# Decay totals with the pairs innermost, logs 16 places sooner, and the last turn's sums started 8 places sooner, in a fused HGRN2 and serf kernel

## The chip, the cores and the metric

The kernel runs on one core of one Trainium2 chip. The core has five engines with a queue of instructions each: TensorE (PE; its weight loads are shown apart as PEld) for matrix products, VectorE (DVE), ScalarE (ACT) and GpSimd (POOL) for elementwise work, and SyncE (SP), whose queue issues most of the transfers. An engine takes its queue strictly in order and waits at an instruction until what it needs is there. The metric is the device time of one execution in microseconds (us). Before the change it is 604.55 us, the median of three runs (603.59, 604.55 and 605.84).

## The reference

Two blocks follow each other. The first is a gated linear recurrence over 768 positions for 4 batches of 8 heads with 48 channels; its output, laid out as 3072 rows of 384, is the input of the second, a product with a 384 x 2048 matrix, an activation, and a product with a 2048 x 384 matrix. All values are 32-bit floats.

```python
f = 1.0 / (1.0 + np.exp(-f_logit))
for t in range(S):
    state = f[:, :, t, :, None] * state + np.einsum('bhd,bhe->bhde', k[:, :, t], v[:, :, t])
    y[:, :, t] = np.einsum('bhd,bhde->bhe', q[:, :, t], state)
...
h = x @ w_in
sp = np.maximum(h, 0.0) + np.log1p(np.exp(-np.abs(h)))
g = h * erf(sp)
return g @ w_out
```

## The kernel before

**Chunks.** The 3072 positions are 24 chunks of 128, each of two halves of 64 (`C`). A chunk's recurrence is turned into matrix products. The logits of f, one position per partition, are clamped (L392) and become logarithms, `log(1 + exp(-logit))`, by an exp (L400) and a ln (L401) on ACT; the two need another function table than the tanh of the activation, so the table is loaded ahead of them (L380) and the other one again at the next tanh (shown at L163 or L719). PE sums the logarithms over the positions of each half (L424, or L435 in four tiles). `decays` takes two exps of these sums on ACT (both L444): `dp`, the decay since the half's start, and its inverse, `kd`. DVE multiplies q by dp (L457) and k by kd (L464). PE transposes both (L484, L494), ACT and DVE copy the transposes out (L504, L124), PE forms the scores (L576) and the products of k and v (L565), the scores are masked (L601, L603), and PE forms the output (L650), which ACT copies out as input of the second block (L661).

**Totals.** The last position of each half of dp, 8 heads x 48 channels, is the decay over that half. The state needs it along the partitions: 64 rows for each head of a pair, four pairs side by side, as `Tall[:, g, c, :]` with 128 partitions and four values. `dp` is stored as [position, head, channel padded to 64]. For chunks 0 to 5 PE moves the totals over: `sum_totals` loads a pair of heads of dp as weights and multiplies them by two columns of the identity (L584), and DVE copies the result to Tall (L590). From chunk 6 on `send_totals` issues transfers on SP's queue, one for each pair and half, eight a chunk, each of 128 values of 4 bytes to 128 partitions (L451). DVE scales the state by Tall (L539, L542) and POOL copies it beside v (L547).

**Blocks and turns.** Two chunks are a block of 256 rows; there are 12. Blocks 0 to 2 and the loading and rounding of the weights are in an early part whose order is written out by hand (`EARLY`). From then on a loop over turns (`it` = 2 to 11) orders the work. A turn is a stream of PE's products, the places, counted as `s`. From turn 4 to turn 10 it has 104 places: first the 56 (`n_o`) of `project(it - 2)`, the second product of an earlier block, then the 48 (`n_h`) of `hiddens(it + 1)`, the first product of a later one (L765), in four groups of four 128-wide tiles. Each place is one product, two records in the profile. Turn 11 is `project` three times, 168 places. Whatever else is due at a place is issued after its product, to the queues of the engines.

**A product of a block.** `project` uses seven half-size products instead of eight (the Strassen and Winograd scheme), which need sums and differences of blocks of the hidden values: `sum_h`, four DVE operations (L803) a group, one for each `sum_step`. Its order: 12 places of products 1, 2, 6 for groups 0 and 1, 16 places of 5, 7, 3, 4, then 12 places of 1, 2, 6 for groups 2 and 3. Here, at place 40, ACT copies product 1 (L932) and DVE adds the pair 2 and 6 (L924), which ends the use of the first of two pairs of PSUM banks. After 16 more places of 5, 7, 3, 4 three more L924 end that of the second. The next product, or the first groups of the hidden values, takes these pairs of banks in turn and waits for them.

**The activation.** Each group of hidden values is copied out of PSUM by ACT (L777) and then goes through seven steps: exp (L160), two tanh terms (L163 twice), two multiplications on DVE (L168 twice), a last tanh (L719) and a multiplication on DVE (L722). `act_step` advances the two groups in work by one step each. Two buffers `e` exist, so the exp of a group waits for L722 of the group before the last. Act steps are issued at places with `s % 9` equal to 2 or 6 in turns 4 to 10 and at every third place in turn 11.

**What else a turn issues.** At places 67 and 103 a `burst` runs a chunk's PE work of the recurrence in one stretch, with its copies, exps and multiplications behind it, the totals, and then the loads of chunks further on. `load_f` for a block's logits is issued 20 places before the end of a turn, eight transfers (L259). In the next turn `clamp` is issued six places ahead of `logs`:

```python
loads, logits_at = {n - 20: it + 5}, {36: it + 4}
if it == 3:
    loads[6], logits_at = it + 4, {8: it + 3, 34: it + 4}
...
if logits_at.get(s + 6, n_blocks) < n_blocks:
    clamp(logits_at[s + 6], 0, CPB)
if logits_at.get(s, n_blocks) < n_blocks:
    logs(logits_at[s], 0, CPB)
```

There are 12 blocks, so the first of these lines takes effect in turns 4 to 7. The sums of groups 0 to 2 of a block are queued one turn ahead of its product, those of group 3 within it at place 20; in turn 11 the sums of the following block are queued at place 40 of a product (L1202).

Of the kernel before, what the change touches and what calls it, by code (L numbers as in the profile page):

```python
# [47 lines left out]
AF = mybir.ActivationFunctionType  # L48
ALU = mybir.AluOpType
# [21 lines left out]
P = 128  # L71
# [3 lines left out]
def kernel(  # L75
# [133 lines left out]
    dps = [fixed(f"dp{i}", [P, H, DP], pool=fix) for i in range(2)]  # L209
# [230 lines left out]
    def decays(g):  # L440
        ps = dTs.pop(g).rearrange("t n (h d) -> t n h d", d=D)
        for t, scale in ((dps[g % 2], -1.0), (kds[g % 2], 1.0)):
            out = t[:, :, 0:D].rearrange("t (n h) d -> t n h d", n=2)
            nc.scalar.activation(out=out, in_=ps, func=AF.Exp, scale=scale)  # L444

    def send_totals(g):
        dp = dps[g % 2]
        for c in range(2):
            end = C * (c + 1)
            for a in range(HP):  # L450
                nc.sync.dma_start(  # L451
                    out=Tall[:, g, c, a : a + 1],
                    in_=dp[end - 1 : end, 2 * a : 2 * a + 2, :].rearrange("o r d -> o (r d)"),
                )

    def times_q(g):
        nc.vector.tensor_tensor(  # L457
            out=qd[:, :, 0:D], in0=qns[g % NQ][:].rearrange("t (h d) -> t h d", d=D),
            in1=dps[g % 2][:, :, 0:D], op=ALU.mult,
        )  # L460
# [120 lines left out]
    def sum_totals(g):  # L581
        pairs = dps[g % 2][:].rearrange("t (a r) d -> t a (r d)", r=2)
        for a in range(HP):
            nc.tensor.matmul(  # L584
                totals[:, 2 * a : 2 * a + 2], lhsT=pairs[:, a, :], rhs=ident[:, C - 1 : P : C],
                start=True, stop=True,
            )
# [487 lines left out]
    with tc.manual_schedule():  # L1075
# [13 lines left out]
        for t in dps:  # L1089
            nc.vector.memset(t[:, :, D:DP], 1.0)  # L1090
# [53 lines left out]
        for it in range(2, n_blocks):  # L1144
# [3 lines left out]
            loads, logits_at = {n - 20: it + 5}, {36: it + 4}  # L1148
# [10 lines left out]
            for s, _ in enumerate(gen):  # L1159
# [28 lines left out]
                if it < 4:  # L1188
                    step = s % 7 in (1, 4)
                elif it == n_blocks - 1:  # L1190
                    step = s % 3 == 1
                else:
                    step = s % 9 in (2, 6)
# [5 lines left out]
                elif it > 2:  # L1199
                    if s == n - n_h and it < n_blocks - 1:  # L1200
                        to_sum.extend(sum_h(groups[it - 1, gi]) for gi in range(NS))
                    if it == n_blocks - 1 and s % n_o == 40 and s < 2 * n_o:  # L1202
# [5 lines left out]
                    elif s < n_o or s % 3 == 0 or it == n_blocks - 1:  # L1208
                        sum_step()
# [217 lines left out]
```

## Time and profile before

| what | before |
|---|---|
| median of three runs | 604.55 us |
| profiled execution: its time | 603.14 us |
| its span, first to last instruction | 601.4 us |
| mean granted clock of PE | 0.995 |
| PE busy | 581.5 us |
| DVE busy | 429.6 us |
| ACT busy | 382.9 us |
| POOL busy | 103.5 us |
| turns 4, 5, 6, 7 begin at | 230.35, 276.51, 323.20, 368.47 us |
| turn 11 begins at | 540.6 us |

The profile page is one execution. "Busy" is time with an instruction in work; matmuls overlap, so PE's share says how long products were in work, not how well the array was used. A wait is put down to the instruction whose end came last before the waiting one began. The chain of waits follows from the last instruction back to what released it. A line of the timeline has the start in us, the busy time in us, the engine, the line of the kernel, the operation, what it writes and reads, how many instructions were merged, and in brackets the idle time ahead and its releaser. In the list of the instructions that touch a tile, durations are minimum, median and maximum in ns. A place of the second product takes 0.329 us in steady state (18.40 us for 56), one of the first 0.44 us.

### The profile page before, as it was taken

The page shows a single profiled execution, that of the slowest core. Times are in us where ns is not written, and L with a number is a line of the kernel's source. Part 1 is how long each engine was busy: PE and PEld are TensorE (multiplying, and loading weights), DVE is VectorE, ACT ScalarE, POOL GpSimd, SP SyncE. Part 2 cuts the span into 40 slices and gives each one's busy share as a digit, 9 for nine tenths or more (in the row PEclk, how much of TensorE's full clock was granted, in tenths as well). Part 3 has the DMA queues.
Part 4 walks back from the last instruction along what each step waited for, and adds up shares of the span by engine and source line. Part 5 has one row for each costly group of instructions (what it writes and reads, how often), then busy time and mean ns, then how long its engine had stood idle before and what let it go on. Part 6 is the DMA issues. An engine that isn't in the chain of part 4 may idle for free.

```text
span 601.4 us, 14264 instructions
## 1 busy us (share of the span) xinstructions
PE 581.5 (97%) x5939; PEld 507.6 (84%) x5939; DVE 429.6 (71%) x705; ACT 382.9 (64%) x483; POOL 103.5 (17%) x119
## 2 busy tenths in 40 slices
PE   8999999998799999999999999999999999999996
PEld 7787888886455778889988989989989989989996
DVE  5689889976977487596786685697695775647551
ACT  6748859787746876875866766766566646366000
POOL 1230342220404011033031010022142020000000
PEclk9899999999999999999999999999999999999999
DMA  9789974206231241232332323221311000000000
GB/s 186 212 223 255 238 176 97 43 2 158 31 76 28 55 77 19 52 72 33 71 56 34 72 34 51 52 56 27 75 29 20 26 2 1 27 1 2 27 26 31
DMA packets 152678, 41.38 MB, mean 69 GB/s; under 512 B 144416, under 2 KB 147488, under 8 KB 152608
## 3 DMA queue, kind: packets, MB, share of 16 engines
q1 hardware_dynamic: 150384, 39.81, 30.4%
q8 instruction: 49, 0.80, 0.6%
q10 hardware_dynamic: 2224, 0.59, 0.4%
q14 instruction: 21, 0.17, 0.1%
HBM read 35.59 MB, written 4.72 MB: 67 GB/s over the span
## 4 chain that ended last, share of the span: by engine, by line
PE 73%; ACT 12%; DVE 6%; DMA 3%; issue 2%; SPq 2%; POOL 1%; ACTq 0%; DVEq 0%
PE hps L765 33%; PE ops L916 22%; PE ops L865 5%; PE y L650 3%; ACT x L163 3%; PE sc L576 2%; PE sc L565 2%; PE ps_t L494 1%; DMA vt<-in_v_dram 1%; PE ps_t L484 1%; DVE Hg L722 1%; SPq L451 1%; ACT e L160 1%; DVE e L168 1%; ACT Hg L777 1%
## 5 line engine op out<-in xcount | busy, mean ns | idle before, releaser
L765 PE MATMUL hps<-xT,w_in_sb 128*128 128x256 f32 x1152 | 257.5, 381 | 4.5 <-ACT Hg L777 2.8
L765 PEld LDWEIGHTS hps<-xT,w_in_sb 128*128 128x128 f32 x1152 | 216.3, 190 | 37.5 <-ACT Hg L777 3.6
L547 POOL COPY sv<-state 48x192 f32<-48x192 f32 x88 | 87.2, 991 | 337.1 <-DVE state L542 285.2
L168 DVE SCALAR_TENSOR_TENSOR e<-x,e 128x1024 f32<-128x1024 f32 x96 | 117.3, 1221 | 15.0 <-ACT x L163 14.6
L163 ACT ACTIVATE x<-Hg,serf_bias 128x1024 f32<-128x1024 f32 x88 | 97.2, 1138 | 0.2
L160 ACT ACTIVATE e<-Hg 128x1024 f32<-128x1024 f32 x44 | 46.5, 1057 | 67.1 <-DVE Hg L722 67.0
L916 PE MATMUL ops<-wT,Hg 128*128 128x192 f32 x320 | 77.7, 326 | 0.0
L777 ACT COPY Hg<-hps 128x1024 f32<-128x1024 f32 x44 | 44.4, 1009 | 44.6 <-PE hps L765 44.2
L722 DVE TENSOR_TENSOR Hg<-Hg,e 128x1024 f32<-128x1024 f32 x44 | 53.7, 1220 | 24.3 <-ACT e L719 24.3
L916 PE MATMUL ops<-wT,scratch 128*128 128x192 f32 x288 | 67.8, 326 | 0.9 <-DVE scratch L924 0.9
L916 PE MATMUL ops<-w_out_sb,Hg 128*128 128x192 f32 x320 | 65.8, 328 | 0.0
L924 DVE TENSOR_TENSOR scratch<-scratch,ops 128x384 f32<-128x384 f32 (+1 forms) x40 | 19.9, 498 | 52.8 <-ACT scratch L932 41.9
L916 PEld LDWEIGHTS ops<-wT,Hg 128*128 128x128 f32 x320 | 56.3, 190 | 0.1
L603 DVE TENSOR_TENSOR qA<-sc,tri 64x256 f32<-64x256 f32 x68 | 28.7, 422 | 36.5 <-PE sc L576 32.8
L916 PEld LDWEIGHTS ops<-w_out_sb,Hg 128*128 128x128 f32 x320 | 53.8, 190 | 0.5
L719 ACT ACTIVATE e<-e 128x1024 f32<-128x1024 f32 x48 | 50.3, 1048 | 2.8 <-DVE e L168 2.8
L916 PEld LDWEIGHTS ops<-wT,scratch 128*128 128x128 f32 x288 | 50.3, 190 | 1.1 <-issue 1.1
L916 PE MATMUL ops<-w_out_sb,scratch 128*128 128x192 f32 x132 | 32.2, 326 | 0.0
L504 ACT COPY qA<-ps_t 64x512 f32<-64x512 f32 x48 | 27.8, 579 | 4.3 <-PE ps_t L494 2.8
L932 ACT COPY scratch<-ops 128x192 f32<-128x192 f32 x10 | 3.2, 319 | 39.5 <-PE ops L916 39.4
L650 PEld LDWEIGHTS y<-qA,sv 128*32 128x32 f32 x1408 | 21.0, 110 | 8.3 <-issue 6.2
L650 PE MATMUL y<-qA,sv 128*32 128x64 f32 x1408 | 25.0, 221 | 1.0 <-POOL sv L547 0.9
(129 smaller groups left out, 666.8 us busy)
## 6 DMA issues: line engine op xcount, KB each, us to landing
qn<-in_q_dram SPq DMA_DIRECT2D x24, 192.0 KB, 3.9
kn<-in_k_dram SPq DMA_DIRECT2D x23, 192.0 KB, 3.8
vt<-in_v_dram SPq DMA_DIRECT2D x23, 192.0 KB, 3.4
out_dram<-scratch SPq DMA_DIRECT2D x11, 384.0 KB, 2.5
sv<-in_v_dram SPq DMA_DIRECT2D x84, 48.0 KB, 2.5
w_out_sb<-in_moe_w_in_dram SPq DMA_DIRECT2D x4, 768.0 KB, 7.5
Hg<-in_moe_w_in_dram SPq DMA_DIRECT2D x4, 768.0 KB, 6.1
scratch<-in_moe_w_out_dram SPq DMA_DIRECT2D x4, 768.0 KB, 7.2
```

Source lines behind the costliest of these rows:

```text
L160: nc.scalar.activation(out=dst[:], in_=h, func=AF.Exp)
L163: nc.scalar.activation(out=dst[:], in_=h, func=AF.Tanh, bias=serf_bias[:, i : i + 1], scale=SERF_KAB[i][0])
L168: nc.vector.scalar_tensor_tensor(out=e[:], in0=x[:], scalar=SERF_KAB[i][2], in1=e[:], op0=ALU.add, op1=ALU.mult)
L547: nc.gpsimd.tensor_copy(out=svs[g1 % NSV][rows(r), r, c1, :, PAD : PAD + D], in_=state[rows(r)])
L603: nc.vector.tensor_tensor(out=to, in0=sc[half(c), r], in1=tri1[half(c)].unsqueeze(1).broadcast_to((C, HP, C)), op=ALU.mult,)
L650: nc.tensor.matmul(y[M * i : M * (i + 1), kt, half(c)], lhsT=sv[:, r, c, a, o : o + M], rhs=qA[:, r, a, half(c)], start=(c == 0 and n == 0 ...
L719: nc.scalar.activation(out=e[0][:], in_=e[0][:], func=AF.Tanh, scale=SERF_C)
L722: nc.vector.tensor_tensor(out=h, in0=h, in1=e[0][:], op=ALU.mult)
L765: nc.tensor.matmul(hts[blk, gi][:, j, :], lhsT=w_in_sb[:, kt, ft * P : (ft + 1) * P], rhs=xTs[blk][:, kt, :], start=(kt == 0), stop=(kt == ...
L777: nc.scalar.copy(out=gr["h"], in_=hts.pop((blk, gi))[:])
L865: nc.tensor.matmul(ops[:, tt, 0:d_model], lhsT=gr["h"][:, j, tt * P : (tt + 1) * P], rhs=w_out_sb[:, ft, :], start=(ft == 0), stop=(ft == ...
L916: nc.tensor.matmul(place[n], lhsT=x[:, j, :], rhs=y, start=(gi == 0 and j == 0 and n in first), stop=(gi == n_g - 1 and j == 1), skip_grou ...
```

## The change

Three parts. First, `dp` is stored as [position, head of a pair, channel padded to 64, pair], the four pairs innermost. The totals of a half are then 128 x 4 values in the order of Tall, and one transfer of 16 bytes to each of 128 partitions moves them: two transfers a chunk instead of eight. The exp that writes dp (the first L444), the multiplication that reads it for q (L457) and the weight loads of `sum_totals` (L584) now step by four values (16 bytes) from one channel to the next; the padding is set to one as before. Second, in turns 4 to 7 `logs` is issued at place 20 and `clamp` at place 14, where it was 36 and 30. Third, in turn 11 the sums of the following block are queued at place 32 of a product, not 40, and no act steps are issued in the last eight of a product's 56 places; the sum steps have the same bar, which acts together with two other conditions in the same line.

```diff
-    dps = [fixed(f"dp{i}", [P, H, DP], pool=fix) for i in range(2)]
+    dps = [fixed(f"dp{i}", [P, 2, DP, HP], pool=fix) for i in range(2)]
...
     def decays(g):
-        ps = dTs.pop(g).rearrange("t n (h d) -> t n h d", d=D)
-        for t, scale in ((dps[g % 2], -1.0), (kds[g % 2], 1.0)):
-            out = t[:, :, 0:D].rearrange("t (n h) d -> t n h d", n=2)
-            nc.scalar.activation(out=out, in_=ps, func=AF.Exp, scale=scale)
+        ps = dTs.pop(g)
+        nc.scalar.activation(
+            out=dps[g % 2][:, :, 0:D, :].rearrange("t r d (n a) -> t n a r d", n=2),
+            in_=ps.rearrange("t n (a r d) -> t n a r d", r=2, d=D), func=AF.Exp, scale=-1.0,
+        )
+        nc.scalar.activation(
+            out=kds[g % 2][:, :, 0:D].rearrange("t (n h) d -> t n h d", n=2),
+            in_=ps.rearrange("t n (h d) -> t n h d", d=D), func=AF.Exp,
+        )
 
     def send_totals(g):
-        dp = dps[g % 2]
         for c in range(2):
             end = C * (c + 1)
-            for a in range(HP):
-                nc.sync.dma_start(
-                    out=Tall[:, g, c, a : a + 1],
-                    in_=dp[end - 1 : end, 2 * a : 2 * a + 2, :].rearrange("o r d -> o (r d)"),
-                )
+            nc.sync.dma_start(
+                out=Tall[:, g, c, :],
+                in_=dps[g % 2][end - 1 : end].rearrange("o r d a -> o (r d) a"),
+            )
 
     def times_q(g):
         nc.vector.tensor_tensor(
-            out=qd[:, :, 0:D], in0=qns[g % NQ][:].rearrange("t (h d) -> t h d", d=D),
-            in1=dps[g % 2][:, :, 0:D], op=ALU.mult,
+            out=qd[:, :, 0:D].rearrange("t (a r) d -> t a r d", r=2),
+            in0=qns[g % NQ][:].rearrange("t (a r d) -> t a r d", r=2, d=D),
+            in1=dps[g % 2][:, :, 0:D, :].rearrange("t r d a -> t a r d"), op=ALU.mult,
         )
...
     def sum_totals(g):
-        pairs = dps[g % 2][:].rearrange("t (a r) d -> t a (r d)", r=2)
+        last = dps[g % 2][:].rearrange("t r d a -> t (r d) a")
         for a in range(HP):
             nc.tensor.matmul(
-                totals[:, 2 * a : 2 * a + 2], lhsT=pairs[:, a, :], rhs=ident[:, C - 1 : P : C],
+                totals[:, 2 * a : 2 * a + 2], lhsT=last[:, :, a], rhs=ident[:, C - 1 : P : C],
                 start=True, stop=True,
             )
...
         for t in dps:
-            nc.vector.memset(t[:, :, D:DP], 1.0)
+            nc.vector.memset(t[:, :, D:DP, :], 1.0)
...
-            loads, logits_at = {n - 20: it + 5}, {36: it + 4}
+            loads, logits_at = {n - 20: it + 5}, {20: it + 4}
...
                 elif it == n_blocks - 1:
-                    step = s % 3 == 1
+                    step = s % 3 == 1 and s % n_o < 48
...
-                    if it == n_blocks - 1 and s % n_o == 40 and s < 2 * n_o:
+                    if it == n_blocks - 1 and s % n_o == 32 and s < 2 * n_o:
                         blk = n_blocks - 2 + s // n_o
                         to_sum.extend(sum_h(groups[blk, gi]) for gi in range(NS))
                     if it == 3:
                         if s % 2:
                             sum_step()
-                    elif s < n_o or s % 3 == 0 or it == n_blocks - 1:
+                    elif s < n_o or s % 3 == 0 or it == n_blocks - 1 and s % n_o < 48:
                         sum_step()
```

## The prediction

> **What bounds the kernel now.** I read the page first. TensorE (PE) is busy in 581.5 of 601.4 us at full clock, so a change can win only PE's idle time (19.9 us, some 5 of it after the last product) or lengthen PE's own stream.
>
> ```profile
> PE 581.5 (97%) x5939; PEld 507.6 (84%) x5939; DVE 429.6 (71%) x705; ACT 382.9 (64%) x483; POOL 103.5 (17%) x119
> ...
> PE   8999999998799999999999999999999999999996
> ```
>
> Next, the waits of PE alone: who, for whom, us in total, times, longest. All L924 waits together are 1.7 us; the plain idle of 1.1 us at L494 has no releaser.
>
> ```profile
> PE ps_t L494 <- ACT xT L661: 1.9, 2, 1.1
> ...
> PE ps_t L494 <- issue: 1.1, 1, 1.1
> ...
> PE ops L916 <- DVE scratch L924: 0.9, 1, 0.9
> PE hps L765 <- DVE scratch L924: 0.8, 2, 0.6
> ```
>
> The L765 waits on L924 stand at 249.34 (0.59) and 387.05 (0.18), at the end of a product. The chain of waits for turn 4 shows why (start, us, what): ScalarE (ACT) works through the logs, two table loads and a tanh before it reaches the copy L932, whose product PE had finished at about 243.5 (start 230.35 + 40 places of 0.329).
>
> ```profile
> 242.90 1.28 ACT L380
> ...
> 244.19 0.85 ACT lt L400
> ...
> 245.07 0.84 ACT lt L401
> ...
> 245.92 1.28 ACT L163
> 247.20 0.01 issue
> 247.21 1.15 ACT x L163
> 248.36 0.03 issue
> 248.38 0.33 ACT scratch L932
> ```
>
> Last, VectorE (DVE) and PE at the end of the first product of the last turn: a product of an activation (L722) and sums (L803) precede the last three L924, and PE waits 0.88.
>
> ```profile
> 559.83 1.22 DVE L722 TENSOR_TENSOR Hg<-Hg,e 128x1024 f32<-128x1024 f32 x1
> ...
> 562.10 1.52 DVE L924 TENSOR_TENSOR scratch<-scratch,ops 128x384 f32<-128x384 f32 x3
> ...
> 563.76 0.56 PE L916 MATMUL ops<-wT,scratch 128*128 128x192 f32 x2 [0.88 <-DVE scratch L924]
> ```
>
> **What the Trainium skill says.** (1) "SBUF — State Buffer", Door 1: memory lines are 16 bytes; two hits in a line are needed for full speed, and each step to a new line pays; yet it also calls a stride of 4 fp32 free. The new layout strides by exactly 4 fp32, one hit a line. The trace has only a stride of 8 bytes: ACT L344 takes 924 ns where the unstrided L400 of the same 768 takes 844; DVE L359 takes 559, L350 unstrided 557. (2) "ScalarE: Activation LUTs", What ACT_TABLE_LOAD costs: 1283 ns a load, plus a drain; the trace has 1283 and no gap beyond 0.02 us. (3) "TensorE: Matmul & The Clock Gate", LDWEIGHTS: columns / 1.2 ns. The trace agrees in slope: 190 ns for 128 columns, 110 for 32, 0.83 a column.
>
> **The change part by part.**
>
> *Totals in two transfers.* 18 chunks go by DMA: 144 issues become 36. One issue takes 0.60 us, with its gap 0.64; SyncE's queue (SP) saves 6 × 0.64 = 3.9 us a chunk, 69 us in all. What follows it there (sv, vt, qn, kn, then lt) starts 3.9 us sooner. Who waited for these? In PE's list nobody; DVE's waits on lt lie before 64 us, and the first totals go out at 73.8. Tall is read two chunks later. Worth: 0, hidden by the look-ahead of the loads. If that cover were gone, 3.9 us a chunk at most.
>
> *Its price: the stride of 16 bytes.* It appears in three places, none with such a row in the trace. (a) Weights of L584: 48 loads, chunks 0 to 5, 192 ns, 8 in 0.98 us, so PE goes at their pace. Free: 0. One line per column at half pace: 128 × 0.83 = 107 ns more, 48 times = 5.1 us, all in PE's stream, 11 to 75 us, where L603 and L601 wait for L584. (b) ACT's exp into dp, 24 × 492 ns. Free: 0; halved: 384 × 0.83 = 0.32 us each. (c) DVE's L457, 24 × 550 ns. Free: 0; halved: 0.40 us. Nothing suggests a gain: the same elements pass. I take 0 for all three, since stride 8 costs DVE nothing and ACT 9%, but keep both ends. In a burst (b) and (c) put ACT and DVE 0.7 us later, which only the margins below feel. The memsets, twice 165 ns, are equal.
>
> *Logs at place 20.* Turns 4 to 7 (3 has its own places). The work on ACT is the same 1.28 + 0.84 + 0.84 + 1.28 = 4.27 us. The clamp L392 (0.55) moves to place 14, ahead of the sums of the fourth group; it needs lt, issued at place n − 20 a turn before (for turn 4 at 219 to 224.5, 2.5 to land), long there. Behind the logs in ACT's queue stand four steps of activations; behind the clamp, DVE's sums, shifted 0.47, which PE reads from place 36 on, 2.5 us later. Turn by turn, with the trace's durations and the rule that the next e (L160) waits for L722 of the group before:
> - Turn 4: logs run 237.6 to 241.9, L719 ends 242.9, L722 244.2, L160 245.3, two L163 247.4, L932 247.7, L924 248.3. PE wants 248.75. The wait of 0.59 goes, margin 0.4.
> - Turn 5: logs 284.0 to 288.3, two L163 290.5, L719 291.4, L722 292.7, L160 293.8, L932 294.1 (before: 291.35), L924 294.7; PE wants 294.9. Worse by 2.8 us, and by luck still hidden, margin 0.2. The copies L777 and L661 of the next burst come 0.9 to 1.2 later and just meet L494 at 302.4.
> - Turn 6: L932 at 337.0 instead of 338.4; no wait before or after.
> - Turn 7: logs 375.9 to 380.2, L163, L719 382.3, L722 383.5, L160 384.6, L163 385.7, L932 386.0, L924 386.6; PE wants 386.87. The 0.18 goes, margin 0.2.
>
> Sum: −0.77 us.
>
> *Last turn.* The 12 sums of the next block start at place 32, not 40. Eight now run ahead of the first L924: from L168 at 552.07, two sums to 554.1, L722 and L168 to 556.4, six sums to 558.67, L924 to 559.22 (before: 556.4). PE wants that bank at 558.83: a new wait of 0.43. Then four sums to 560.7, and the three L924 to 562.3, since the step with L722 moves from place 49 to 58. PE reaches place 68 at 559.26 + 12 × 0.325 = 563.16, not 563.76: −0.6. In the second product DVE is idle from 565 to 573, L924 ended 1.8 us before PE wanted it: 0.
>
> Sum: −0.59 − 0.18 − 0.6 = −1.4 us. The profiled execution took 603.14 (span 601.4 and 1.7 around it), so 601.8; against the median of the three runs, 604.55, it is **603.2 us**.
>
> **The rivals.**
> - *The 16-byte stride costs half pace* (slower). Place: L584's weight loads, then exp and L457. Price: about 4 of the 5.1 us (idle PE of 0.4 to 0.6 us before 40 us swallows some) plus about 1.5 us where ACT and DVE are already late (startup, 155.3, turn 3). The margins of turns 4, 5 and 7 go too, three waits of 0.3 to 0.5, eating the gain of 1.4: 604.55 + 5.5 = 610.0. For it: the skill's two hits. Against: the rows with 8 bytes. It decides from some 4.4 us of loss. PE's part alone: 604.55 − 1.4 + 4 = 607.2; ACT and DVE alone: about 606.
> - *The waits move instead of going* (no change). Turn 5 stands 0.2 us from a wait and the last turn gets one of 0.43; another 0.5 us in each undoes the gain: 604.5.
> - *SP's queue matters more than its waits show* (faster). The 1.1 us idle in the midst of L494 at 322.9, with no releaser, falls in a stretch of eight totals issues; were such stretches to hold up PE's instructions and disappear, 1 to 2 us more: 601.2. For it: the coincidence; against: one case in 18.
> - *The change does not do what it says.* `s < n_o or ...` still lets sums run in the last places of the first product; only the activation step is barred there. The sums are gone because they are used up at place 43. Counted above; no time of its own.
>
> **How the numbers follow.** Forecast 0.47, own range 601.8 to 604.6; moved waits 0.10 at 604.5; SP 0.15 at 601.2; stride in part 0.10 at 606 to 607; stride in full 0.18 at 610.0. About 0.5%, 3.0 us, is what a measurement of this kernel can tell from no change: below 601.5 lie most of SP and a little of the forecast, 0.18; above 607.6 the full stride, part of the partial one and what I do not see, 0.27; between them 0.55. The range of 601.0 to 609.5 leaves out about half of SP's case below and half of the full stride's above, some 0.16.
>
> **What the profile after would show.** L584's weight loads at 192 ns and 8 in 0.98 us (at 300, the stride rival holds); exp into dp at 0.49 and L457 at 0.55; two totals issues a chunk; no wait of L765 on L924 near 249 and 387, none above 0.2 near 295; the clamp near place 14; in the last turn eight sums ahead of L924, a wait of 0.4 at 558.8 and none 12 places on. Wrong would be: a new wait in turn 5, a longer stream before 75 us, or loads that, 3.9 us sooner, meet others.

## The result, and the profile after

| | before | after |
|---|---|---|
| median | 604.94 us (603.59 to 605.84, 4 runs) | 614.71 us (614.48 to 615.51, 4 runs) |
| profiled execution: time, span | 603.14, 601.4 us | 614.48, 612.8 us |
| mean granted clock of PE | 0.995 | 0.987 |
| PE busy | 581.5 us | 592.7 us |

The ratio is 1.0166, with a 95% interval of 1.0143 to 1.0188: the change makes the kernel about 10 us slower. The forecast was 603.2 us, its range 601.0 to 609.5.

First the page of the changed kernel. PE's busy time has grown by 11.2 us and the span by 11.4, so nearly all of the loss is in PE's own stream and not in its waits. The row of the granted clock shows a part of it: three of the first seven slices stand at 8.

```profile
PE 592.7 (97%) x5939; PEld 517.7 (84%) x5939; DVE 438.1 (71%) x705; ACT 390.3 (64%) x483; POOL 95.7 (16%) x119
...
PE   8999999998999998999999999999999999999996
...
PEclk9889989999999999999999999999999999999999
```

The kernel before has only one such slice:

```profile
PEclk9899999999999999999999999999999999999999
```

Next, the instructions that write or read `dp`: engine, operation, tiles, count, then the shortest, the median and the longest in ns. First the kernel before, then the changed one (its lines are two to four numbers off: L588 was L584, L454 was L451, L442 was L444, L460 was L457).

```profile
L451 SPq DMA_DIRECT2D Tall<-dp x144: 476/599/1697, 73.8 to 445.4; - x144
L584 PEld LDWEIGHTS sc<-ident,dp x48: 186/192/192, 11.0 to 74.5; 128*128 128x128 f32 x48
L584 PE MATMUL sc<-ident,dp x48: 170/251/272, 11.1 to 74.5; 128*128 128x2 f32 x48
L444 ACT ACTIVATE dp<-ps_d x24: 472/491/506, 7.5 to 440.3; 128x384 f32<-128x384 f32 x24
L457 DVE TENSOR_TENSOR qd<-qn,dp x24: 540/550/987, 8.0 to 442.9; 128x384 f32<-128x384 f32 x24
```

```profile
L588 PEld LDWEIGHTS sc<-ident,dp x48: 307/329/332, 11.8 to 82.6; 128*128 128x128 f32 x48
L588 PE MATMUL sc<-ident,dp x48: 287/372/395, 11.9 to 82.7; 128*128 128x2 f32 x48
L454 SPq DMA_DIRECT2D Tall<-dp x36: 476/577/640, 81.2 to 453.4; - x36
L442 ACT ACTIVATE dp<-ps_d x24: 858/876/915, 7.7 to 452.0; 128x384 f32<-128x384 f32 x24
L460 DVE TENSOR_TENSOR qd<-qn,dp x24: 830/877/972, 8.6 to 454.9; 128x384 f32<-128x384 f32 x24
```

All three places where a stride of 16 bytes now stands have become slower: the weight load of the totals by 137 ns (192 to 329), the exp by 385 (491 to 876), the multiplication by q by 327 (550 to 877). The transfers are down from 144 to 36, as the change says. PE's stream around the second chunk's totals shows what the load costs there (start, us, what), before and after:

```profile
18.71 1.05 PE L584 MATMUL sc<-ident,dp 128*128 128x2 f32 x8
```

```profile
21.36 2.03 PE L588 MATMUL sc<-ident,dp 128*128 128x2 f32 x8
```

Over the six chunks these stretches are 6.1 us before (two of 0.95, four of 1.05) and 11.96 after (two of 1.92, four of 2.03): 5.9 us more. The shift of like points against before grows in just this part: 0.8 us at the first totals (11.07 to 11.87), 2.65 at the second, 5.4 at the fourth (33.21 to 38.57), 7.3 at the last (73.69 to 81.02). From 9.9 at 99 us (99.06 to 108.92) it rises only to 11.4 at the end.

The waits of PE in the changed kernel answer to those shown of before (us in total, times, longest):

```profile
PE ps_t L498 <- ACT xT L665: 1.9, 2, 1.1
...
PE ops L920 <- issue: 0.9, 1, 0.9
...
PE ps_t L498 <- issue: 0.6, 1, 0.6
PE hps L769 <- DVE scratch L928: 0.5, 1, 0.5
...
PE ops L920 <- DVE scratch L928: 0.2, 1, 0.2
```

In this list the wait of turn 4 on the column sums is gone. One of 0.5 is left, in turn 7 at 397.75, and 0.2 in the last turn where there were 0.9. The 1.1 us of plain idle at L494 is 0.6 here, with another of 0.9 at the product L920. But the weight loads ahead of the products L769 wait for the same sums as long as before, first the kernel before, then the changed one:

```profile
PEld hps L765 <- DVE scratch L924: 1.4, 2, 0.9
```

```profile
PEld hps L769 <- DVE scratch L928: 1.4, 3, 0.8
```

Before, these are turn 4 (0.89) and turn 7 (0.47); now they are turn 4 (0.41, at 259.81), turn 5 (0.20, at 305.52) and turn 7 (0.79). So the three together wait as long as the two did before: what the sooner logs gain here, the slower exp and multiplication take (without the sooner logs the waits are longer still, see the layout alone below).

The copy L936 of turn 5 came when it was computed to: at 304.56 it is 17.6 us after the start of the turn's product (286.91). The product L769 starts at 305.52, with the 0.20 at its weight load but no wait of its own.

```profile
303.48 1.06 ACT L160 ACTIVATE e<-Hg 128x1024 f32<-128x1024 f32 x1 [1.29 <-DVE Hg L726]
304.56 0.32 ACT L936 COPY scratch<-ops 128x192 f32<-128x192 f32 x1
```

In the last turn eight sums stand ahead of the first L928, three L928 follow in one stretch, and the multiplication L726 comes after them. The wait of 0.88 us for these three is gone; instead PE waits 0.21 us for the first L928, twelve places sooner:

```profile
570.33 0.54 DVE L928 TENSOR_TENSOR scratch<-scratch,ops 128x384 f32<-128x384 f32 x1
...
572.38 1.52 DVE L928 TENSOR_TENSOR scratch<-scratch,ops 128x384 f32<-128x384 f32 x3
573.82 1.22 DVE L726 TENSOR_TENSOR Hg<-Hg,e 128x1024 f32<-128x1024 f32 x1
```

```profile
570.92 0.92 PE L920 MATMUL ops<-w_out_sb,Hg 128*128 128x192 f32 x4 [0.21 <-DVE scratch L928]
```

One thing in this profile had not been thought of at all, the clock. By stretches of the changed kernel (length; busy us and instructions of PE, PEld, DVE, ACT and POOL; then the granted clock), right behind the last chunk's totals:

```profile
84.00:84.50 0.50, 0.50 (x23) 0.35 (x24) 0.47 (x3) 0.18 (x1) 0.00 (x0) 0.85 0.00 0
84.50:87.50 3.00, 3.00 (x30) 2.38 (x22) 2.97 (x5) 1.72 (x4) 2.62 (x2) 0.50 0.26 47
87.50:88.00 0.50, 0.50 (x4) 0.39 (x3) 0.50 (x1) 0.00 (x0) 0.50 (x2) 0.73 0.27 41
88.00:90.00 2.00, 2.00 (x11) 1.77 (x10) 1.90 (x4) 0.74 (x1) 1.53 (x4) 1.00 0.81 156
```

For 3.4 us the clock is exactly half, although PE is busy all the time. Such a dip costs (0.15 + 0.27) x 0.5 + 0.50 x 3.0 = 1.7 us of full clock. The changed kernel's profile has four before 160 us (from 16.1, 33.2, 84.4 and 152.6), the kernel before one (from 21.7), each of the same length. Three more of 1.7 us and the 5.9 us of the loads sum to 11.0 us; PE's busy time has grown by 11.2. Both profiles have another dip at their end, behind the last product, where it costs nothing.

### The profile page after: what moved, and what is told of

The parts are those of the page before. It is cut to its first block, busy times and chain, and to the rows that moved or that the text cites. A ratio compares the mean times of both kernels' runs of the same rounds, so it can differ in the third digit from the quotient of the medians.

```text
span 612.8 us, 14111 instructions
## 1 busy us (share of the span) xinstructions
PE 592.7 (97%) x5939; PEld 517.7 (84%) x5939; DVE 438.1 (71%) x705; ACT 390.3 (64%) x483; POOL 95.7 (16%) x119
## 4 chain that ended last, share of the span: by engine, by line
PE 73%; ACT 12%; DVE 10%; issue 2%; POOL 1%; DMA 1%; ACTq 0%; DVEq 0%; POOLq 0%; SPq 0%
PE hps L769 33%; PE ops L920 21%; PE ops L869 5%; PE y L654 3%; ACT x L163 3%; DVE Hg L726 2%; PE sc L580 2%; DVE e L168 2%; PE sc L569 2%; PE sc L588 2%; PE busy L408 1%; PE ps_t L488 1%; ACT e L160 1%; POOL sv L551 1%; PE ps_t L498 1%
## 5 line engine op out<-in xcount | busy, mean ns | idle before, releaser
L769 PE MATMUL hps<-xT,w_in_sb 128*128 128x256 f32 x1152 | 260.1, 384 | 4.9 <-ACT Hg L781 3.5
L769 PEld LDWEIGHTS hps<-xT,w_in_sb 128*128 128x128 f32 x1152 | 218.4, 192 | 38.6 <-ACT Hg L781 4.3
L551 POOL COPY sv<-state 48x192 f32<-48x192 f32 x88 | 78.7, 894 | 352.7 <-DVE state L546 290.7
L920 PE MATMUL ops<-wT,Hg 128*128 128x192 f32 x320 | 77.6, 326 | 0.0
L726 DVE TENSOR_TENSOR Hg<-Hg,e 128x1024 f32<-128x1024 f32 x44 | 53.8, 1223 | 28.4 <-ACT e L723 28.4
L920 PE MATMUL ops<-wT,scratch 128*128 128x192 f32 x288 | 67.8, 326 | 0.0
L920 PE MATMUL ops<-w_out_sb,Hg 128*128 128x192 f32 x320 | 66.1, 329 | 1.1 <-issue 0.9
L920 PEld LDWEIGHTS ops<-wT,Hg 128*128 128x128 f32 x320 | 56.3, 190 | 0.1
L920 PEld LDWEIGHTS ops<-w_out_sb,Hg 128*128 128x128 f32 x320 | 53.8, 190 | 2.1 <-issue 1.0
L920 PEld LDWEIGHTS ops<-wT,scratch 128*128 128x128 f32 x288 | 50.3, 190 | 0.3 <-issue 0.3
L928 DVE TENSOR_TENSOR scratch<-scratch,ops 128x384 f32<-128x384 f32 (+1 forms) x40 | 19.9, 498 | 41.7 <-ACT scratch L936 26.7
L920 PE MATMUL ops<-w_out_sb,scratch 128*128 128x192 f32 x132 | 32.2, 326 | 0.0
L442 ACT ACTIVATE dp<-ps_d 128x384 f32<-128x384 f32 x24 | 21.1, 881 | 14.6 <-PE ps_d L435 6.4
L936 ACT COPY scratch<-ops 128x192 f32<-128x192 f32 x10 | 3.2, 319 | 39.2 <-PE ops L920 39.1
```

Source lines behind the costliest of these rows:

```text
L551: nc.gpsimd.tensor_copy(out=svs[g1 % NSV][rows(r), r, c1, :, PAD : PAD + D], in_=state[rows(r)])
L726: nc.vector.tensor_tensor(out=h, in0=h, in1=e[0][:], op=ALU.mult)
L769: nc.tensor.matmul(hts[blk, gi][:, j, :], lhsT=w_in_sb[:, kt, ft * P : (ft + 1) * P], rhs=xTs[blk][:, kt, :], start=(kt == 0), stop=(kt == ...
L920: nc.tensor.matmul(place[n], lhsT=x[:, j, :], rhs=y, start=(gi == 0 and j == 0 and n in first), stop=(gi == n_g - 1 and j == 1), skip_grou ...
```

## The experiments

Four theories were set against each other. **A**: the stride of 16 bytes is the whole loss. **A1** and **A2** divide it: mostly the weight loads, or mostly exp and multiplication. **B**: the moved logs or sums carry a part. **C**: the lost clock belongs to the kernel as it is and not to the slow loads. Times are medians. Each ratio is that of the record, to the kernel before, run beside it on the same chip (its median there was 603.85 to 604.94), and differs in places by a little over 0.1% from the quotient of the two medians. Differences are these ratios and their 95% intervals, less one, times 604.5 us.

**The layout alone (`layout`).** The changed kernel with logs and sums where they were before:

```diff
-            loads, logits_at = {n - 20: it + 5}, {20: it + 4}
+            loads, logits_at = {n - 20: it + 5}, {36: it + 4}
...
-                    step = s % 3 == 1 and s % n_o < 48
+                    step = s % 3 == 1
...
-                    if it == n_blocks - 1 and s % n_o == 32 and s < 2 * n_o:
+                    if it == n_blocks - 1 and s % n_o == 40 and s < 2 * n_o:
...
-                    elif s < n_o or s % 3 == 0 or it == n_blocks - 1 and s % n_o < 48:
+                    elif s < n_o or s % 3 == 0 or it == n_blocks - 1:
```

> The layout of dp and its two transfers alone; logs and last turn's sums stay where the kernel before has them. Theory A (the stride of 16 bytes is the whole cost): the weight loads of the totals take 329 ns, the exponentials of dp 876 ns and the multiplication by q 877 ns, as in the changed kernel, and the time is that of the changed kernel plus the 1.4 us which I credited to the two moves: 615 to 617 us, a ratio of 1.017 to 1.020. Theory B (the moved logs or sums carry part of the cost): 605 to 611 us, the rest of the 10 us comes with the moves.

Measured: 617.54 us, ratio 1.0202 (1.0176 to 1.0228), so 12.2 us more. The layout by itself loses more than the whole change, as A says, and a little more than the 615 to 617 us that A gave; B is out. The waits on the column sums in turns 4 and 7, 0.59 and 0.18 us before, have grown in its profile. That fits exp and multiplication, which by their durations take 0.7 us longer in each chunk:

```profile
260.15 2.21 PE L769 MATMUL hps<-xT,w_in_sb 128*128 128x256 f32 x9 [1.07 <-DVE scratch L928]
...
398.73 5.45 PE L769 MATMUL hps<-xT,w_in_sb 128*128 128x256 f32 x24 [0.88 <-DVE scratch L928]
```

**The moves alone (`rest`).** The reverse: the kernel before with those four lines as the change has them, and `dp`, exp and eight transfers as before.

```diff
-            loads, logits_at = {n - 20: it + 5}, {36: it + 4}
+            loads, logits_at = {n - 20: it + 5}, {20: it + 4}
...
-                    if it == n_blocks - 1 and s % n_o == 40 and s < 2 * n_o:
+                    if it == n_blocks - 1 and s % n_o == 32 and s < 2 * n_o:
```

> The logs at place 20 and the last turn's sums ahead of its last places, with dp and the eight transfers as before. Theory A: 1.4 us less than before, as forecast (0.77 for the logs, 0.6 for the sums): 603.0 to 604.0 us against 604.9, ratio 0.997 to 0.9985. Theory B: 3 us or more above before, 608 to 611 us.

Measured: 602.63 us, ratio 0.9965 (0.9947 to 0.9984), 2.1 us less (1.0 to 3.2). The forecast's gain of 1.4 lies inside. The waits of turns 4 and 7 are gone from its profile and only this one on the column sums is left:

```profile
PE ops L916 <- DVE scratch L924: 0.2, 1, 0.2
```

Layout and moves add up to the change: 12.2 - 2.1 = 10.1, measured 10.0.

**The old layout for the first six chunks (`from6`).** The changed kernel, but chunks 0 to 5, whose totals PE sums, keep the old order within the same memory (the multiplication by q too, not shown; two memsets on DVE set the padding anew when the order changes):

```diff
+    def flat_dp(g):
+        return dps[g % 2][:].rearrange("t r d a -> t (r d a)").rearrange("t (h d) -> t h d", h=H)
...
+        if g < TOTALS:
+            nc.scalar.activation(
+                out=flat_dp(g)[:, :, 0:D].rearrange("t (n h) d -> t n h d", n=2),
+                in_=ps.rearrange("t n (h d) -> t n h d", d=D), func=AF.Exp, scale=-1.0,
+            )
...
-        last = dps[g % 2][:].rearrange("t r d a -> t (r d) a")
+        pairs = flat_dp(g).rearrange("t (a r) d -> t a (r d)", r=2)
```

> The changed kernel, except that chunks 0 to 5 (those whose totals TensorE sums) keep dp in the old order; from chunk 6 on dp has its pairs innermost and leaves in two transfers. Theory A with the cost in the fill: the 48 weight loads are back at 192 ns and the first six exponentials and multiplications back at 0.5 us, so at most the 18 later chunks' slower exponentials (0.39 us each) and multiplications (0.32 us each) are left, which the turns mostly hide: 603.5 to 605.5 us. Theory C (the loss of clock comes with the kernel, not with the slow weight loads): the 4 us beyond the loads' own 5.9 us stay, 607 to 609 us. If the strided work of the turns costs its full 18 x 0.7 us: 612 us or more.

Measured: 604.77 us, ratio 1.0000 (0.9979 to 1.0021). So 10 us come back when six of 24 chunks are spared; the loss is made in the early part, and with it goes the loss of clock (below), so C is out as well. Against the run with the moves alone 2.1 us are left; the two intervals, -1.3 to 1.3 and -3.2 to -1.0, overlap by a little. What differs is exp and multiplication at 16 bytes in the 18 later chunks, and their two transfers in place of eight. Part of the cost can be seen: a wait of 0.5 us on the column sums stands in this profile, as in the changed kernel's, where the moves alone leave none at that kind of product.

**Which access.** For this the order of the columns must not change any value. So these kernels take the exponentials at a scale of 0, and `dp` starts as ones; then a single access can be strided and the rest kept. The base (`ones_base`):

```diff
-        for t, scale in ((dps[g % 2], -1.0), (kds[g % 2], 1.0)):
+        for t in (dps[g % 2], kds[g % 2]):
             out = t[:, :, 0:D].rearrange("t (n h) d -> t n h d", n=2)
-            nc.scalar.activation(out=out, in_=ps, func=AF.Exp, scale=scale)
+            nc.scalar.activation(out=out, in_=ps, func=AF.Exp, scale=0.0)
...
-            nc.vector.memset(t[:, :, D:DP], 1.0)
+            nc.vector.memset(t[:], 1.0)
```

> Left out: the decays themselves. Both exponentials take a scale of 0, so dp and kd begin as ones and the order of dp's columns changes no value; layout, transfers, logs and sums are those of the kernel before. It is the base for the three that follow, which change one access each. Every theory: the durations of all instructions stay, and so does the time, 604 to 606 us.

Measured: 604.42 us, ratio 1.0001 (0.9983 to 1.0019). Leaving the decays out changes nothing that can be measured. Then the weight loads alone (`ones_ldw`):

```diff
-        pairs = dps[g % 2][:].rearrange("t (a r) d -> t a (r d)", r=2)
+        last = dps[g % 2][:].rearrange("t h d -> t (h d)").rearrange("t (x a) -> t x a", a=HP)
...
-                totals[:, 2 * a : 2 * a + 2], lhsT=pairs[:, a, :], rhs=ident[:, C - 1 : P : C],
+                totals[:, 2 * a : 2 * a + 2], lhsT=last[:, :, a], rhs=ident[:, C - 1 : P : C],
```

> The base with ones, and in it only the 48 weight loads of the totals read dp at a step of 16 bytes; the exponential and the multiplication by q stay at 4 bytes. Theory A1 (the weight loads are most of the cost): the loads take 329 ns, eight of them 1.95 us in place of 1.0, six times 0.95 is 5.7 us, and with the clock that is lost behind these slow streams 7 to 9 us above the base. Theory A2 (the exponentials and multiplications, which the fill's chain passes through, are half of it or more): 3 to 6 us above the base.

Measured: 611.72 us, ratio 1.0121 (1.0097 to 1.0145), 7.3 us above the base. The loads have the changed kernel's duration while exp and multiplication stay at 490 and 550 ns:

```profile
L584 PEld LDWEIGHTS sc<-ident,dp x48: 307/329/333, 12.1 to 81.6; 128*128 128x128 f32 x48
```

Then exp and multiplication both, the loads left alone (`ones_expq`):

```diff
+        wide = dps[g % 2][:].rearrange("t h d -> t (h d)").rearrange("t (r d a) -> t r d a", r=2, a=HP)
+        nc.scalar.activation(
+            out=wide[:, :, 0:D, :].rearrange("t r d (n a) -> t n a r d", n=2),
+            in_=ps.rearrange("t n (a r) d -> t n a r d", r=2), func=AF.Exp, scale=0.0,
+        )
...
-            in1=dps[g % 2][:, :, 0:D], op=ALU.mult,
+            in1=dps[g % 2][:].rearrange("t h d -> t (h d)").rearrange(
+                "t (r d a) -> t a r d", r=2, a=HP
+            )[:, :, :, 0:D], op=ALU.mult,
```

> The base with ones, and in it only the exponentials that write dp and the multiplications by dp work at a step of 16 bytes; the weight loads stay at 4 bytes. The exponential takes 876 in place of 491 ns and the multiplication 877 in place of 550 ns, 24 times each. Theory A1: 2 to 4 us above the base (six times 0.7 us in the fill, part of it hidden, and little in the turns). Theory A2: 6 us or more above it.

Measured: 607.59 us, ratio 1.0052 (1.0033 to 1.0070), 3.1 us above the base, with 876 ns an exp and 871 a multiplication at the median and 192 a load. A1 holds: seven tenths of the two together are the loads'. The sum of 7.3 and 3.1 is 10.4, somewhat below the layout's 12.2 but within the intervals.

The two of these apart (`ones_exp_only` and `ones_q_only`), with the upper and the lower half of that diff:

> Left out: the decays, as in the other runs with ones. In it only the exponential that writes dp works at a step of 16 bytes. In the fill the totals' products wait for it and in some chunks the PE is idle until it ends: 6 x 0.39 us is 2.3 us at most there, and the 18 others lie in the turns beside the PE: 1 to 3 us above the base of ones.

> Left out: the decays, as in the other runs with ones. In it only the multiplication of q by dp reads dp at a step of 16 bytes. It follows the exponential and the PE's transposes of q wait for it (2.3 us in the kernel before, at one place), so 6 x 0.32 us is 1.9 us at most in the fill: 0.5 to 2 us above the base of ones. If the exponential and the multiplication cover each other, the two alone sum to more than the 3.2 us of both together.

Measured: 607.44 us, 1.0047 (1.0029 to 1.0064), for the exp, which took 874 ns at a median; 607.30 us, 1.0032 (1.0010 to 1.0055), for the multiplication, 868 ns. That is 2.8 and 1.9 us over before, more together than the 3.1 of both at once. That they cover each other would fit, but the intervals are too wide to show it, and each of the two also lost some 1.3 us more clock time than the kernel before beside it (table below), against 0.4 with both at once.

**Half the stride (`ones_ldw8`).** The base with ones, with weights 8 bytes apart:

```diff
-        pairs = dps[g % 2][:].rearrange("t (a r) d -> t a (r d)", r=2)
+        last = dps[g % 2][:].rearrange("t h d -> t (h d)").rearrange("t (n x a) -> t n x a", n=2, a=2)
...
-                totals[:, 2 * a : 2 * a + 2], lhsT=pairs[:, a, :], rhs=ident[:, C - 1 : P : C],
+                totals[:, 2 * a : 2 * a + 2], lhsT=last[:, a // 2, :, a % 2], rhs=ident[:, C - 1 : P : C],
```

> The base with ones, and only the 48 weight loads of the totals read dp at a step of 8 bytes. If the price of a step grows with the bytes that are passed over: about 60 ns a load more than the unstrided 192 (half way to the 329 of 16 bytes), some 3 us above the base. If a step of 8 bytes is read at full pace, as the VectorE's was in the kernel before: 192 ns a load, and the base's time within 0.3%.

```profile
L584 PEld LDWEIGHTS sc<-ident,dp x48: 193/196/197, 11.5 to 75.3; 128*128 128x128 f32 x48
```

Measured: 604.67 us, ratio 1.0008 (0.9996 to 1.0020). A load costs 4 ns more at 8 bytes and 137 more at 16. The price is not in proportion to the step: nearly all of it comes between 8 and 16 bytes. A step of 12 was not tried.

**The moves where they were wanted (`tuned`).** The kernel before, logs at place 20 only in the two turns whose wait they can take away, sums from place 34:

```diff
-            loads, logits_at = {n - 20: it + 5}, {36: it + 4}
+            loads, logits_at = {n - 20: it + 5}, {20 if it in (4, 7) else 36: it + 4}
...
-                    step = s % 3 == 1
+                    step = s % 3 == 1 and s % n_o < 48
...
-                    if it == n_blocks - 1 and s % n_o == 40 and s < 2 * n_o:
+                    if it == n_blocks - 1 and s % n_o == 34 and s < 2 * n_o:
```

> The kernel before with logs at place 20 in turns 4 and 7 alone (the two turns whose column sums made the PE wait) and the last turn's sums begun at place 34 of each product, none of them in the last eight. Theory A: turn 4's 0.59 us and turn 7's 0.18 us of wait go, turn 5 keeps its place 36 and so no new wait, and the last turn's 0.88 us becomes 0.3 us: 1.3 us below before, 603.3 to 603.9 us. Theory B: not below before, 604.5 to 606 us.

Measured: 602.65 us, ratio 0.9961 (0.9946 to 0.9977). It is the moves alone once more; no wait on the column sums is left in its profile, and what that adds is below what the intervals resolve.

**Two pairs innermost (`pairs_by_two`).** If the price comes between 8 and 16 bytes, a layout with two pairs innermost keeps half of the saved transfers for nothing. `Tall` takes the same order:

```diff
-    dps = [fixed(f"dp{i}", [P, H, DP], pool=fix) for i in range(2)]
+    dps = [fixed(f"dp{i}", [P, 2, 2, DP, 2], pool=fix) for i in range(2)]
...
+        nc.scalar.activation(
+            out=dps[g % 2][:, :, :, 0:D, :].rearrange("t a r d n -> t n (a r) d"),
+            in_=ps, func=AF.Exp, scale=-1.0,
+        )
...
-            for a in range(HP):
+            for a in range(2):
                 nc.sync.dma_start(
-                    out=Tall[:, g, c, a : a + 1],
-                    in_=dp[end - 1 : end, 2 * a : 2 * a + 2, :].rearrange("o r d -> o (r d)"),
+                    out=Tall[:, g, c, 2 * a : 2 * a + 2],
+                    in_=dp[end - 1 : end, a].rearrange("o r d n -> o (r d) n"),
                 )
```

> Two pairs innermost in dp and in Tall in place of four (a step of 8 bytes), four transfers a chunk in place of eight or two, and the moves of the run tuned (logs at place 20 in turns 4 and 7, the last turn's sums from place 34). Theory A (a step of 8 bytes costs next to nothing, and nobody waits for the transfers): the loads take 196 ns, the exponential of dp some 530 and the multiplication some 550, the time is that of the run tuned within 0.3%, 602 to 604 us. If fewer transfers are worth something to anyone: 600 to 601.5 us. If 8 bytes cost the ScalarE or the VectorE half of what 16 do: 604.5 us or more.

```profile
L456 SPq DMA_DIRECT2D Tall<-dp x72: 492/598/1294, 73.7 to 440.9; - x72
L592 PEld LDWEIGHTS sc<-ident,dp x48: 193/196/197, 11.6 to 74.4; 128*128 128x128 f32 x48
...
L442 ACT ACTIVATE dp<-ps_d x24: 515/527/565, 8.1 to 438.5; 128x384 f32<-128x384 f32 x24
L462 DVE TENSOR_TENSOR qd<-qn,dp x24: 530/550/995, 8.7 to 441.2; 128x384 f32<-128x384 f32 x24
```

Measured: 601.89 us, ratio 0.9965 (0.9952 to 0.9979). The layout is free: 36 ns on an exp, 4 on a load, nothing on the multiplication. And 72 transfers fewer than before are worth nothing that can be measured, since the same moves with all 144 gave 0.9961. This kernel and the two with the moves and the old `dp` beat both the kernel before and the changed one, by what the moves bring.

**The lost clock.** Each run also has a mean granted clock, so one minus the clock, times the span, is the clock time that it lost. A dip behind the last product counts in it too; in the profiles that is up to 1.4 us. The mean over all runs of a kernel:

| kernel | runs | clock time lost, us |
|---|---|---|
| before, beside all the experiments | 154 | 2.4 |
| two pairs innermost; moves where wanted | 15; 22 | 1.8; 2.1 |
| ones: base; loads at 8 bytes | 22; 22 | 2.3; 2.2 |
| moves alone; old layout for six chunks | 15; 14 | 3.1; 3.4 |
| ones: exp and multiplication | 7 | 2.8 |
| ones: exp alone; multiplication alone | 22; 13 | 3.5; 3.4 |
| ones: loads at 16 bytes | 6 | 6.8 |
| layout alone | 6 | 6.2 |
| the changed kernel | 4 | 7.2 |

It is the slow loads that go with the loss: 6.2 to 7.2 us with them, 3.5 or less without. Do they bring it on as slow loads? In the next kernel nothing is strided, but each product of the totals (48 records in the profile) is issued twice (`prod_twice`, and once more as `prod_twice_2`):

```diff
                 totals[:, 2 * a : 2 * a + 2], lhsT=pairs[:, a, :], rhs=ident[:, C - 1 : P : C],
                 start=True, stop=True,
             )
+            nc.tensor.matmul(
+                totals[:, 2 * a : 2 * a + 2], lhsT=pairs[:, a, :], rhs=ident[:, C - 1 : P : C],
+                start=True, stop=True,
+            )
```

> The kernel before with each of the 48 products of the totals issued twice in a row (the second gives the same values): the PE is held 1.0 us longer at each of the six places, as by the slow loads, but with loads at full pace. If the clock that is lost is a consequence of slow loads: 6.0 us above before, 610 to 611 us, mean clock 0.995. If being late at these six places is what counts, whatever makes it late: 7 to 9 us above before, and the clock dips as in the run ones_ldw (0.989).

Measured: 612.86 us, ratio 1.0152 (1.0110 to 1.0195), 7.1 us of clock lost on the mean. So the slow load as such is not needed: 1.0 us more at each of the six places, with loads at full pace (192 ns), costs 9.2 us (6.6 to 11.8).

Two readings were left. These products move only 2 columns each, so that the array has next to nothing to do for 2 us; or whatever stands behind them is merely late. The last kernel (`dense`) gives the second product 64 columns, written where nobody reads:

```diff
+            nc.tensor.matmul(
+                sc_all[:, 1, HP * (C + D) : 512], lhsT=tri[:], rhs=tri[:, 0:C], start=True, stop=True,
+            )
```

> The kernel before, and after each of the 48 products of the totals one product of 64 columns that nobody reads, in place of the second product of 2 columns of the run prod_twice: the PE is held as long, 1.0 us more at each of the six places. If the little work of the 2-column products is what costs the clock: the loss of clock stays near the 2.4 us of the kernel before, and the time is 6 us or less above it (608 to 611). If being late is what costs it: lost clock of 6 to 7 us and 8 to 10 us above before, as with the products twice.

> The repeat of the products issued twice, on the chip of the dense run: 7 to 11 us above before, 7 us of clock lost on a mean over its runs.

Measured: with 64 columns 608.89 us, ratio 1.0082 (1.0050 to 1.0115), 4.4 us of clock lost; with the products twice again 610.03 us, ratio 1.0105 (1.0061 to 1.0150), 6.4 lost; the kernel before beside them lost 2.6. The dense products lie between, and the intervals of the two ratios overlap, so these two runs alone don't decide.

The profiles do. Their clock is either full or half, and before the last product the dips of one kernel start whole multiples of 3.413 us apart (in the changed kernel 5, 15 and 20 of them). So each profile can be cut into windows of that length, and for each window the work of PE's array can be estimated from the shapes in the trace: a product's columns, times the share of the 128 x 128 array that its weights fill, spread evenly over the product's time. In the changed kernel the window ahead of the dip at 84.4 us holds little else than this:

```profile
81.02 2.03 PE L588 MATMUL sc<-ident,dp 128*128 128x2 f32 x8
82.98 0.65 PE L654 MATMUL y<-qA,sv 128*32 128x64 f32 x32
83.56 0.66 PE L488 MATMUL ps_t<-ident,qd 128*128 128x128 f32 x4
84.15 0.95 PE L654 MATMUL y<-qA,sv 128*32 128x64 f32 x32
```

That is 8 x 2 = 16 columns for the totals, 32 x 64 on a quarter of the array, which counts as 512, 4 x 128 = 512 for the transposes, and some 140 from products that reach in at its two ends: 1,183. The median window holds 4,033.

The sixteen profiles have 2,780 windows between 4 us and the last product. The 28 with the least work, 1,403 columns or less, are exactly the 28 that a dip follows; the other 2,752 hold 1,427 or more. In five of the 28 PE was busy from end to end, while a window with PE busy for only 1.43 us, but with 1,620 columns, has no dip behind it (`layout`, from 161.2 us). So it is little work in the array that goes ahead of a dip, and not being late. The totals bring a window below the mark when they are stretched and fall mostly into one window: three of the changed kernel's four dips follow such a window. Its fourth, at 152.6, follows a wait of 2.0 us at L769. In the profile of `dense` the window with the last chunk's totals holds 1,760 columns and no dip follows. This is a count over the runs that there are, and none was made to test it; if a product's columns are booked at its start alone, the 28 lie among the lowest 61 windows and no longer apart. Three windows in the first microsecond hold less than 1,403 and no dip follows them.

## Why the prediction was wrong

**The step that failed is "I take 0 for all three"**, the price of the stride of 16 bytes. Measured, the three cost 7.3 us (the weight loads) and 3.1 us (exp and multiplication), and the whole layout 12.2 us. The ground for the 0 was that a stride of 8 bytes costs DVE nothing and ACT 9%. That ground is true, and the runs bear it out (196 ns a load, 527 an exp, 550 a multiplication at 8 bytes), but it doesn't carry over to 16. The prediction had quoted the Trainium skill, "SBUF — State Buffer", Door 1, with two statements that pull apart here: memory lines of 16 bytes with two hits in each for full speed, and a stride of 4 fp32 as free. The first of them agrees with the measurements, 8 bytes (two hits a line) almost free and 16 bytes (one hit) dear; the second does not hold for any of the three engines that were measured. That lines are the mechanism is only argued; that the price comes between 8 and 16 bytes is shown.

**The bounds were too low for PE and ACT.** Half pace was reckoned as 107 ns a load, 0.32 us an exp and 0.40 us a multiplication. Measured: 137 ns, 0.385 us and 0.33 us.

**The rival "half pace" named the right accesses and missed the size.** It put PE's part at 4 us, ACT's and DVE's at 1.5, let the gain of 1.4 vanish, and came to 610.0; the result is 614.71. Term by term:
- PE: 4 assumed, 7.3 measured (run with only the loads strided). The loads lengthen PE's stream by 5.9 and not by 5.1, and 4.4 us of clock time more are lost with them (6.8 against 2.4). The two sum to 10.3, so some 3 us of them don't reach the end; the prediction had let idle PE swallow 1.1. How much of the 7.3 is clock and how much is loads, no run separates. But the clock goes with the thin stretches, not with the stride: the products issued twice at full pace cost 9.2 and 6.3 us in their two sets of runs.
- ACT and DVE: 1.5 assumed, 3.1 measured (2.0 to 4.2 over the kernel before).
- The margins: the rival let turns 4, 5 and 7 fall back into waits of 0.3 to 0.5 us each. Turn 7 did, with 0.5 us; in turns 4 and 5 only the weight loads wait, 0.41 and 0.20 us.

The lost clock stands in no term of the prediction. PE's part, with the clock in it, is 3.3 us over the rival's, and that of ACT and DVE 1.6; together that is about the distance from 610.0 to 614.71 (the moves' gain and the 1.8 us by which the layout exceeds the sum of its parts about cancel). The range ended at 609.5 because it was drawn to cut off half of that rival.

**The moves were right.** Sum forecast: -1.4 us; the moves alone gave -2.1 (-3.2 to -1.0). Turn 4's wait is gone, and turn 5's copy came 17.6 us after the start of the turn's product, where 294.1 - 276.5 had been computed. In the last turn the eight sums ahead of the first L928, and the three L928 ahead of L726, came as described; of the new wait of 0.43 there were 0.21. In the changed kernel turn 7 kept a wait, which fits its margin of 0.2 against the 0.7 us that exp and multiplication take longer; with the moves alone it is gone. So the gain was read rightly for a `dp` without a price, and in the changed kernel the logs' part of it was eaten by the later exp and multiplication, as the rival had said.

**Two transfers for eight: 0, right as far as it was tried.** Four for eight made no difference that can be measured (0.9965 beside 0.9961). Two for eight came only together with the stride of 16 bytes, and its effect by itself wasn't tried.

**The other rivals.** SP's queue as a hidden brake has nothing for it: the idle stretch at L494 shrank from 1.1 to 0.6 us, but another of 0.9 turned up elsewhere, the layout alone with its two transfers has 1.3 us at the same line, and half of the transfers gone won nothing. "The waits move instead of going" describes turns 5 and 7 and the last turn, for less than 1 us, and decides nothing. "The change does not do what it says" didn't come true: it did all it says.

**The sign and the range.** 0.27 was given to slower by over 0.5%, and this happened. The forecast of least price was taken as likeliest though the trace had no row for three strided accesses, one of which lies wholly on the bounding engine; and a first bound, half pace, was treated as the worst. An access form with no row would have deserved a range that goes beyond it.

## What to carry to other kernels

Before a layout is turned for the sake of transfers, look up who reads it and on which engine: here 108 transfer issues on a queue for which nobody waited were saved, and 48 weight loads on the engine that sets the time paid for it. Before four 4-byte values are interleaved, try two: a step of 8 bytes was free on PE and DVE here and nearly so on ACT. Where a layout serves two stages, spare the stage that pays: with the old order for the first six chunks the loss of the change was gone, though the later chunks gained nothing by theirs. And a stretch of narrow products on PE can cost twice: its own time, and the dip behind it.

## What the runs showed of the hardware that was not expected

- A stride of 16 bytes between 4-byte values: 329 for 192 ns on a weight load of 128 columns, 876 for 491 on an ACT exp that writes 384 a partition, 877 for 550 on a DVE multiplication that reads one of two inputs so. A stride of 8 bytes: 196, 527 and 550.
- PE's clock falls to exactly half for 3.41 us at a time, 1.7 us of full clock a dip, behind a window of that length in which the array had little work: 1,403 columns or less by the estimate above, where the median window has 4,033 and 1,427 brought no dip, so some 35%. Busy records of PE don't tell: in five of the 28 windows ahead of a dip PE was busy from end to end. The Trainium skill, "TensorE: Matmul & The Clock Gate", Part 1 on the clock gate, gives the half rate and a free-running window of about 3.4 us, and both agree here; it puts the half rate behind an idle window, which for those five isn't what the trace shows. Lengthening six stretches of 2-column products from 1 to 2 us each raised the clock time lost from 2.4 to between 6.2 and 7.2 us, whether by slow loads or by twice as many. With 64 columns in every second product it was 4.4.
